# Late attention's transposed probabilities travel by way of a scratch in DRAM

## The chip, the cores and the metric

The kernel runs on one core of a Trainium2 chip. The metric is the device time of one execution in microseconds, the median of several runs. A core has a matmul engine (TensorE, PE in the profile; its weight loads are PEld), a vector engine (VectorE, DVE), a scalar engine (ScalarE, ACT), GpSimd (POOL) and SyncE (SP), which issues the transfers of this kernel. Each engine works through its own instructions in order; sixteen DMA engines move the data.

## What is computed

Attention over 4 batches, 8 heads, 576 positions and 64 dimensions a head. Half of the heads see the last 32 positions, the other half every 32nd position back. Two feed-forward layers follow; the second one sends each row to one of 8 experts.

```python
scores = scale * np.matmul(q, k.transpose(0, 1, 3, 2))
mask_local = (rel >= 0) & (rel < stride)                     # stride = 32
mask_strided = (rel >= 0) & (pos[None, :] % stride == pos[:, None] % stride)
scores = np.where(masks, scores, -1e9); attn = softmax(scores)
x = np.matmul(attn, v)                                       # to 2304 rows of 512
r = np.maximum(x @ w_in, 0.0)                                # 512 -> 2048
x = (s * (r * r) + b) @ w_out                                # 2048 -> 512
e_idx = np.argmax(x @ w_gate, axis=1)                        # one of 8 experts a row
out[row] = gate_w * eom * (np.maximum(x @ w1[e], 0.0) @ w2[e])
```

## The kernel before

The 2304 rows are worked in five units (256 and four times 512 rows). Attention is worked in 23 groups (GROUPS). The first nine are done by themselves; the other fourteen, "late attention", are woven into the first feed-forward layer of the first three units. These matmuls (L1095 into the hidden layer, L1129 out of it, with weights split into two parts and three passes) and those of late attention share TensorE.

The order of all instructions is written by a planner (class Order) when the program is built. Each piece of work is a generator that yields `op(engine and assumed time, what it waits for)`; the planner keeps a clock for each engine, picks the piece that can start first, with small penalties (P_ATT2 for attention, P_SPLIT2 for weights), and emits its instructions. All engines then run this order; only real waits move it in time. DMA counts as an engine with a clock of its own, and every DMA of these stages is issued by SP in the planned order. Tokens (Tok) stand for buffers, events (Ev) for data; an event that a transfer sets is assumed to come DMA_LAT (1.8 us) and a further constant after the transfer's assumed end.

A late group is one round. late_scores multiplies q and k, late_mask adds the mask into the tile pr, late_rest takes the maximum, the exponentials (L849, ScalarE) and the normalisation (L852 to L855, VectorE), and transposes 32x32 blocks from pr to prt (L859). The transposed blocks then have to go to other partitions: prt has 128 rows by (pair p of heads, half x of the queries, 32), phs needs 128 rows by (half x, block of keys y, 32). DMAs do that (L867): eight of 32 KB for a full round (nb = 2; groups L and T), four smaller ones for the two P groups (nb = 1). They wait for the token t_ph, that is for the former round's matmuls to have read phs, and the planner assumes 2.55 us times nb for them and DMA_LAT + PH_LAT = 2.6 us behind. Then one piece on TensorE holds the matmuls of phs with v (L884) and the scores of the group after next (L799). Two groups are under way at any time (NPR = 2 tiles pr), but prt, phs, and the tiles of the loaded q and k and of v exist once. So the loads of the next q and k and of the next v (load_qkv, L592) start as soon as a round's matmuls on TensorE have been done, at about the time of the next round's transfers. The weights' loads (L950) are on the same queue until 134 us; stores and loads of later stages (L934, L1227 and L1228, L1245, L1263, L1520) follow.

ev_x of a unit is set when all of its attention has been done; the unit's first feed-forward matmuls wait for it. Where the planner expects TensorE to stand still for longer, it puts in matmuls of no use (filler, L2393).

Of the kernel before, what the change touches and what calls it, by code (L numbers as in the profile page):

```python
# [6 lines left out]
F32 = mybir.dt.float32  # L7
# [31 lines left out]
QB = 64  # L39
# [13 lines left out]
NPR = 2  # L53
QG = 32
NQE = 6
P_CHAIN = -0.35
P_ATT = -0.3
P_QKL = 0.1
P_SPLIT = 0.0
# [61 lines left out]
def dims(g):  # L121

    if GROUPS[g][0] == "L":
        return (QB, LK) if g < NEARLY else (QG, 2 * QG)
    j0, j1, r = part_of(g)
    if g >= NEARLY:
        return r * (j1 - j0), r * j1
    return r * (j1 - j0), QB if GROUPS[g][0] == "P" else r * j1


def span(g):
    kind, b, i0, n = GROUPS[g]
    if kind == "L":
        return b * S + i0 * QB, b * S + (i0 + n) * QB
    j0, j1, _ = part_of(g)
    return b * S + j0 * STRIDE, b * S + j1 * STRIDE
# [62 lines left out]
DMA_LAT = 1.8  # L199
LATE_LAT = 0.8  # L200
PH_LAT = 0.8
# [115 lines left out]
def op(*engs, waits=(), dep=True, on=(), late=0.0):  # L317
    return engs, waits, dep, on, late
# [6 lines left out]
def body(ctx, tc, qkv, w12, moe_s, moe_b, wg, e12, out):  # L325
    nc = tc.nc
# [5 lines left out]
    dram = enter(tc.tile_pool(name="dram", bufs=1, space=DRAM))  # L332
# [23 lines left out]
    prs = [at.tile([P, 1024 // 2], F32, name=f"pr{k}", tag=f"pr{k}", bufs=1) for k in range(NPR)]  # L356
    prt = at.tile([P, 1024 // 2], F32, name="prt", tag="prt", bufs=1)
    phs = at.tile([P, 2, 2, 256], F32, name="phs", tag="phs", bufs=1)
    away = at.tile([P, 2, USZ[AWAY]], F32, name="away", tag="away", bufs=1)
    mh = wp.tile([P, sum(MB[0])], F32R, name="mh", tag="w")  # L360
    x0 = wp.tile([P, KD, USZ[0]], F32, name="x0", tag="w")
# [33 lines left out]
    o = Order()  # L395
# [68 lines left out]
    t_qe, t_qk, t_vv, t_pt, t_ph = Tok(NQE), Tok(1), Tok(1), Tok(1), Tok(1)  # L464
# [108 lines left out]
    for g, (kind, b, i0, n) in enumerate(GROUPS):  # L573
        t0, t1 = span(g)
# [26 lines left out]
    def attn(g):  # L601
# [41 lines left out]
        if g + 1 < len(GROUPS):  # L643
            o.spawn(attn(g + 1), prio=P_ATT if g + 1 < NFIRST else P_ATT1 if g + 1 < NEARLY else P_ATT2, pe=P_ATT)
        m = 2 * n
# [158 lines left out]
    def late_mask(g, sc, toks):  # L804
        kind, b, i0, n = GROUPS[g]
        local = kind == "L"
        nq, w = dims(g)
        m = 2 * n
        sm = at.tile([P, 24], F32, name="sm", tag="sm", bufs=NSM)
        ps4 = prs[g % NPR][:, 0:m * 2 * QG].rearrange("p (h i k) -> p h i k", h=2, k=2 * QG)[:, :, :, 0:w]  # L810
        edge = [i for i in range(n) if local and (i0 + i) % NLB == 0]
        some = [(i, i + 1, ml[:, 2 * QG:4 * QG]) for i in edge]
        for i, j in zip([0] + [i + 1 for i in edge], edge + [n]):
            if i < j:
                some.append((i, j, ml[:, 0:2 * QG] if local else late_m[kind, b]))
        yield op(("DVE", m * w / 960 + 0.15 * len(some)), on=toks)
        for i, j, mask in some:
            nc.vector.tensor_tensor(out=ps4[:, :, i:j], in0=sc[:, :, i:j], in1=mask.unsqueeze(1).unsqueeze(1).to_broadcast([P, 2, j - i, w]), op=ALU.add)
        o.spawn(late_rest(g, sm, ps4), prio=P_ATT2, pe=P_ATT)

    def attn_late(g):
# [4 lines left out]
        if g + 1 < NEARLY + NPR:  # L826
            o.spawn(attn(g + 1), prio=P_ATT2, pe=P_ATT)
        yield from late_mask(g, sc, toks)
# [3 lines left out]
    def late_rest(g, sm, ps4):  # L832
        kind, b, i0, n = GROUPS[g]
        local = kind == "L"
        nq, w = dims(g)
        m = 2 * n
# [8 lines left out]
        for h in range(2):  # L845
            for i in range(n):
# [10 lines left out]
        nb = 2 if w > QG else 1  # L857
        yield op(("DVE", nb * m * QG / 960 + 0.15), waits=[t_pt])
        nc.vector.transpose(out=prt[:, 0:nb * m * QG].rearrange("p (b c q) -> p b c q", b=nb, q=QG),  # L859
                            in_=pr[:, 0:m * 2 * QG].rearrange("p (c b q) -> p b c q", b=2, q=QG)[:, 0:nb])  # L860
        o.free(t_p)
        yield op(("DMA", 2.55 * nb), waits=[t_ph])
        for x in range(2):
            for y in range(nb):
                for p in range(2):
                    a, r = p * QB + x * QG, x * QB + y * QG
                    nc.sync.dma_start(out=phs[r:r + QG, p, x, 0:m * QG], in_=prt[a:a + QG, y * m * QG:(y + 1) * m * QG])  # L867
        t1 = o.fin + DMA_LAT + PH_LAT
        o.free(t_pt, t1)
        ev = Ev()  # L870
        o.set(ev, t1)
        tot = m * nq
# [7 lines left out]
        for i in range(n):  # L880
            for p in range(2):
                for h in range(2):
                    c = (h * n + i) * QG
                    nc.tensor.matmul(out=two[h * D:(h + 1) * D, p, 256 + 2 * i * nq:256 + 2 * (i + 1) * nq], lhsT=vv[:, i, p, h, :],  # L884
                                     rhs=phs[:, p, :, c:c + nq])
        o.free(t_vv)
        o.free(t_ph)
        if nx:
# [3 lines left out]
        for t0, c, z, _ in segs:  # L892
            if local:
                a = t0 - span(g)[0]
# [7 lines left out]
        for z, src, dst, u in runs:  # L902
            if u == AWAY:
# [9 lines left out]
                if local:  # L913
                    a = span(g)[0] - UOF[AWAY]
# [123 lines left out]
    def chain(k, u, h, ev, box):  # L1038
        U = USZ[u]
        held = k < CUT  # L1040
        yield op(("ACT", U / 1200 + 0.18), waits=[t_r] + ([t_w] if held and k % 3 == 0 else []))
        r = mx.tile([P, UMAX], F32, name="r", tag="r", bufs=NR)[:, 0:U]
        nc.scalar.activation(out=r, in_=h, func=AF.Relu)  # L1043
        to = r
        if held:
            if k % 3 == 0:
                plain[k // 3] = wp.tile([P, 3, U + 2], F32, name="gw", tag="w")
                nc.gpsimd.memset(plain[k // 3][:, :, U:U + 2], 1.0)
            gt = plain[k // 3][:, k % 3, :]
            to = gt[:, 0:U]  # L1050
        yield op(("DVE", U / 960 + 0.15), ("ACT", U / 1200 + 0.19, P_SQ))
        if o.eng == "DVE":
            nc.vector.tensor_tensor(out=to, in0=h, in1=r, op=ALU.mult)
        else:
            nc.scalar.activation(out=to, in_=r, func=AF.Square)  # L1055
        o.free(t_l1)
        if held:
            o.free(t_r)
            box.append(gt)
            o.set(ev)  # L1060
            return
        yield op(("ACT", U / 1200 + 0.19), waits=[t_g])
        gt = mx.tile([P, 2, UMAX], F32R, name="g", tag="g", bufs=NG)
        if u == CU:
            nc.gpsimd.memset(gt[:, 0, U:U + 2].bitcast(F32), 1.0)
            nc.gpsimd.memset(gt[:, 1, U:U + 2].bitcast(F32), 0.0)
        nc.scalar.activation(out=gt[:, 0, 0:U], in_=r, func=AF.Copy)  # L1067
        yield op(("DVE", U / 960 + 0.15))
        nc.vector.tensor_sub(out=gt[:, 1, 0:U], in0=r, in1=gt[:, 0, 0:U].bitcast(F32))  # L1069
        o.free(t_r)  # L1070
        box.append(gt)
        o.set(ev)
# [4 lines left out]
    def moe1():  # L1077
        def first_layer(k, u, fc):
# [22 lines left out]
            ev, box = Ev(), []  # L1101
            o.spawn(chain(k, u, h, ev, box), prio=P_CHAIN)
            return u, fc, ev, box
# [67 lines left out]
    def run(n):  # L1171
        while n and todo[1] is not None:
            yield todo[1]
            todo[1] = next(todo[0], None)
            n -= 1
# [184 lines left out]
    def combine1(u, q, hn, bank, box, m, r, ev0, ev1):  # L1360
# [8 lines left out]
        def c11():  # L1369
            yield op(("SP", 0.0), waits=[m["M2"]], dep=False)  # L1370
            yield op(("ACT", hn / 1200 + 0.2))
            nc.scalar.activation(out=rr[:, 0], in_=bank["a"], func=AF.Relu)
            o.free(t_l1)
            yield from square(rr[:, 0], rr[:, 0], hn)
            yield op(("SP", 0.0), waits=[t_g])
            g = mx.tile([P, 2, UMAX], F32R, name="g", tag="g", bufs=NG)
            box[0].append(g)
            yield from high_low(rr[:, 0], g[:, :, 0:hn], hn)

        def c12():  # L1380
            yield op(("DVE", w), waits=[m["M3"]], dep=False)
            nc.vector.tensor_tensor(out=rr[:, 1], in0=bank["c"], in1=su[:, 1], op=ALU.add)
            o.free(t_l1)
            o.free(t_su)
            yield from square(rr[:, 1], rr[:, 1], hn)
            yield from high_low(rr[:, 1], box[0][0][:, :, hn:2 * hn], hn)
            o.free(t_rr)
            o.set(ev0)
# [3 lines left out]
        o.set(r["u2"])  # L1392
        o.spawn(c11(), prio=P_CHAIN)
        yield op(("DVE", w), waits=[m["M7"]])
# [4 lines left out]
        o.set(r["c22"])  # L1399
        o.spawn(c12(), prio=P_CHAIN)  # L1400
        yield op(("DVE", w), waits=[m["M4"]])
# [10 lines left out]
    def both_rows(k, u, fc, prev):  # L1412
# [41 lines left out]
        yield from product("M6", "S2", "T2", "b", [t_l1], True)  # L1454
        o.spawn(combine1(u, q, hn, bank, box, m, r, ev0, ev1), prio=P_CHAIN)
        yield from run(1)
# [429 lines left out]
    def combine(hn, ps3, box, m, r, done):  # L1886
# [11 lines left out]
        def c11():  # L1898
            yield op(("SP", 0.0), waits=[m["M2"]], dep=False)
            yield from rise(a, h0, 0, hn, done["h0"])  # L1900
            o.free(t_l1)
# [16 lines left out]
        o.set(r["c22"])  # L1918
        o.spawn(c11(), prio=P_CHAIN)
        o.spawn(c12(), prio=P_CHAIN)  # L1920
        yield op(("DVE", w), waits=[m["M4"]])
# [474 lines left out]
    with tc.manual_schedule():  # L2396
# [4 lines left out]
        o.spawn(load_w64(0), after=False)  # L2401
        o.spawn(attn(0), prio=P_ATT, after=False)
        o.spawn(masks(1), after=False)
# [106 lines left out]
```

## Time and profile before

| | us |
|---|---|
| median of 3 runs | 662.09 (661.8 to 662.46) |
| the profiled execution | 662.37 |
| its span in the trace | 660.60 |
| TensorE busy in it | 651.9 |
| VectorE / ScalarE / GpSimd busy | 426.6 / 312.8 / 38.8 |
| late attention's transfers (L867), first and last issue | 72.5 and 245.8 |

The profile is one execution on the core. All times in it are microseconds from the start of the span; the profiled execution's own time has 1.77 us around the span. A row of the timeline has the start, the length and the engine, and merges like instructions that follow one another (x12). The length of a merged row runs to the end of its last instruction, so the pace is read from start to start.

### The profile page before, as it was taken

What the parts mean: (1) busy time and instruction counts of PE and PEld (TensorE: products, weight loads), DVE (VectorE), ACT (ScalarE), POOL (GpSimd) and SP (SyncE); (2) the same over time, 40 slices, a digit from 0 to 9 for tenths busy, and PEclk for the clock granted to TensorE, in tenths of its full rate; (3) what the DMA queues carried; (4) which work ended last, traced back from release to release, by engine and by line L of the source; (5) the groups of instructions that cost most, each with busy time, mean ns of one, the idle gap of its engine ahead of it and who ended that gap; (6) DMA issues with size and microseconds to landing.
All of it is one profiled execution on the core that took longest, in us unless ns stands there. A gap on an engine that the chain in (4) does not pass through costs nothing. (4 is left out here: it accounts for less than half of the span.)

```text
span 660.6 us, 14155 instructions
## 1 busy us (share of the span) xinstructions
PE 651.9 (99%) x5424; PEld 570.0 (86%) x5424; DVE 426.6 (65%) x1001; ACT 312.8 (47%) x848; POOL 38.8 (6%) x135
## 2 busy tenths in 40 slices
PE   7999999999999999999999999999999999999997
PEld 6888888899878888898899889988899999998996
DVE  5898868776545557566575767887687566535540
ACT  4876865677566444353243464543322423314311
POOL 7650000000000000000000000000000000000000
PEclk9999999999999999999999999999999999999999
DMA  8982356673544232112211242333220660910201
GB/s 312 405 334 96 112 209 208 207 245 103 177 152 169 81 106 65 49 48 97 87 50 42 64 152 68 116 97 96 96 65 2 177 237 14 327 44 16 81 1 66
DMA packets 40823, 83.81 MB, mean 127 GB/s; under 512 B 6701, under 2 KB 20142, under 8 KB 39986
## 3 DMA queue, kind: packets, MB, share of 16 engines
q1 hardware_dynamic: 40658, 82.87, 37.2%
q8 instruction: 43, 0.70, 0.5%
q14 instruction: 26, 0.21, 0.1%
q0 software_dynamic: 96, 0.02, 0.0%
HBM read 64.11 MB, written 15.63 MB: 121 GB/s over the span
## 5 line engine op out<-in xcount | busy, mean ns | idle before, releaser
L1095 PE MATMUL h<-xsl,w 128*128 128x512 f32 (+1 forms) x492 | 109.5, 369 | 0.0
L1129 PE MATMUL bk<-g,w 128*128 128x512 f32 (+1 forms) x480 | 105.5, 368 | 0.0
L1190 PE MATMUL bk<-g,w 128*128 128x512 f32 x396 | 102.2, 393 | 0.0
L1095 PEld LDWEIGHTS h<-xsl,w 128*128 128x128 f32 x492 | 84.8, 188 | 15.6 <-issue 0.4
L1968 PE MATMUL bk<-w,ht 128*128 128x512 f32 x384 | 96.0, 391 | 0.0
L1129 PEld LDWEIGHTS bk<-g,w 128*128 128x128 f32 x480 | 83.0, 188 | 14.7
L1190 PEld LDWEIGHTS bk<-g,w 128*128 128x128 f32 x396 | 69.9, 188 | 11.6
L1968 PEld LDWEIGHTS bk<-w,ht 128*128 128x128 f32 x384 | 68.6, 188 | 11.6
L1043 ACT ACTIVATE r<-h 128x512 f32<-128x512 f32 (+1 forms) x48 | 25.3, 528 | 62.5 <-PE h L1095 59.5
L1069 DVE TENSOR_TENSOR g<-r,g 128x512 fp32r<-128x512 f32 (+1 forms) x41 | 26.0, 633 | 42.6 <-ACT g L1067 42.2
L1442 PEld LDWEIGHTS h<-xsl,w 128*128 128x128 f32 x336 | 45.5, 190 | 3.8 <-issue 0.2
L1442 PE MATMUL h<-xsl,w 128*128 128x256 f32 x336 | 47.0, 283 | 0.0
L1873 ACT ACTIVATE ht<-h 128x256 fp32r<-128x256 f32 x24 | 9.2, 385 | 73.2 <-PE h L2010 47.0
L849 ACT ACTIVATE pr<-pr,sm 128x64 f32<-128x64 f32 (+2 forms) x102 | 32.8, 322 | 0.3
L1914 DVE TENSOR_TENSOR dd<-h,su 128x256 f32<-128x256 f32 x16 | 6.8, 424 | 29.5 <-PE h L2010 29.4
L1356 ACT ACTIVATE g<-dd 128x512 fp32r<-128x512 f32 x16 | 10.1, 631 | 31.5 <-DVE dd L1349 31.5
L1067 ACT ACTIVATE g<-r 128x512 fp32r<-128x512 f32 (+1 forms) x41 | 23.9, 583 | 1.7
L1055 ACT ACTIVATE r<-r 128x512 f32<-128x512 f32 (+1 forms) x41 | 23.9, 584 | 1.1
L2010 PE MATMUL bk<-x,wc 128*128 128x256 f32 x168 | 24.4, 281 | 0.0
L1442 PE MATMUL h<-xsl,s 128*128 128x256 f32 x168 | 24.3, 279 | 0.0
L1442 PEld LDWEIGHTS h<-xsl,s 128*128 128x128 f32 x168 | 22.6, 188 | 1.3
L1938 ACT ACTIVATE ob<-bk,scl 128x512 f32<-128x512 f32 x17 | 11.7, 689 | 23.5 <-PE bk L1968 22.8
(306 smaller groups left out, 1132.7 us busy)
## 6 DMA issues: line engine op xcount, KB each, us to landing
raw<-w SPq DMA_DIRECT2D x32, 512.0 KB, 6.9
qkv<-qkv SPq DMA_DIRECT2D x14, 512.0 KB, 4.7
xr<-xd SPq DMA_DIRECT2D x9, 512.0 KB, 4.7
qkv<-qkv SPq DMA_DIRECT2D x8, 544.0 KB, 6.3
out<-ob SPq DMA_DIRECT2D x17, 256.0 KB, 2.1
xd<-x SPq DMA_DIRECT2D x4, 1024.0 KB, 4.2
sraw<-sd SPq DMA_DIRECT2D x16, 256.0 KB, 2.7
wraw<-e SPq DMA_DIRECT2D x16, 256.0 KB, 3.0
```

The lines of the kernel that those rows point to most:

```text
L849: nc.scalar.activation(out=ps4[:, h, i, :], in_=ps4[:, h, i, :], func=AF.Exp, scale=0.125, bias=v[2][:, j:j + 1], accum_out=v[1][:, j:j + 1])
L1043: nc.scalar.activation(out=r, in_=h, func=AF.Relu)
L1055: nc.scalar.activation(out=to, in_=r, func=AF.Square)
L1067: nc.scalar.activation(out=gt[:, 0, 0:U], in_=r, func=AF.Copy)
L1069: nc.vector.tensor_sub(out=gt[:, 1, 0:U], in0=r, in1=gt[:, 0, 0:U].bitcast(F32))
L1095: nc.tensor.matmul(out=h, lhsT=w_t[2 * fc][:, a, c * P:(c + 1) * P], rhs=xt(u, c, x), start=(c == 0 and n == 0), stop=(c == KD - 1 and n = ...
L1129: nc.tensor.matmul(out=acc[pu][c], lhsT=w_t[2 * pf + 1][:, a, c * P:(c + 1) * P], rhs=gt[:, x, 0:cols(pu)], start=(first and n == 0), stop ...
L1190: nc.tensor.matmul(out=acc[pu][c], lhsT=w_t[2 * pf + 1][:, a, c * P:(c + 1) * P], rhs=pbox[0][:, x, 0:cols(pu)], start=(begin and i == 0), ...
L1442: nc.tensor.matmul(out=out_, lhsT=weights(x, a, c), rhs=o_place(u, b)[y][:, c], start=(first and c == 0 and n == 0), stop=(name in ("M2", ...
L1938: nc.scalar.activation(out=ob, in_=src, func=AF.Copy, scale=scl[:, i:i + 1])
L1968: nc.tensor.matmul(out=acc2[s, t][0], lhsT=box[k][:, x, t * P:(t + 1) * P], rhs=w_t["p", 2 * f + 1][:, a, :], start=(f == 0 and n == 0), s ...
L2010: nc.tensor.matmul(out=banks[to], lhsT=t[:, a, off + c * P:off + (c + 1) * P], rhs=x2[s, b][:, y, c, :], start=(first and c == 0 and n == ...
```

## The change

The blocks go from prt to a scratch tile in DRAM (one for each of the two tiles pr) by two writes, one for each pair of heads, and from there to phs by four reads (two for a P group). The two indices in phs change places, and the matmul reads it accordingly. The writes wait for nothing but the transposed tile; prt is given free when the writes have landed; the reads wait for them and for t_ph. The planner's assumed times are new: 0.75 us for the writes and RB = 1.5 us for the reads, each with DMA_LAT + 0.3 us behind.

```diff
+RB = 1.5
...
+    ptd = [dram.tile([2, QG, 2, 2, 256], F32, name=f"ptd{k}") for k in range(NPR)]
...
         o.free(t_p)
-        yield op(("DMA", 2.55 * nb), waits=[t_ph])
+        yield op(("DMA", 0.75))
+        pd_ = ptd[g % NPR]
+        c = m * QG
+        for p in range(2):
+            nc.sync.dma_start(out=pd_.rearrange("x k b p c -> (x k) b p c")[:, 0:nb, p, 0:c],
+                              in_=prt[p * QB:(p + 1) * QB, 0:nb * c].rearrange("q (b c) -> q b c", b=nb))
+        t1 = o.fin + DMA_LAT + 0.3
+        o.free(t_pt, t1)
+        ev = Ev()
+        o.set(ev, t1)
+        yield op(("DMA", RB), waits=[t_ph, ev])
         for x in range(2):
-            for y in range(nb):
-                for p in range(2):
-                    a, r = p * QB + x * QG, x * QB + y * QG
-                    nc.sync.dma_start(out=phs[r:r + QG, p, x, 0:m * QG], in_=prt[a:a + QG, y * m * QG:(y + 1) * m * QG])
-        t1 = o.fin + DMA_LAT + PH_LAT
-        o.free(t_pt, t1)
+            for b in range(nb):
+                nc.sync.dma_start(out=phs[x * QB + b * QG:x * QB + (b + 1) * QG, x, :, 0:c], in_=pd_[x, :, b, :, 0:c])
+        t1 = o.fin + DMA_LAT + 0.3
...
-                                     rhs=phs[:, p, :, c:c + nq])
+                                     rhs=phs[:, :, p, c:c + nq])
```

## Rows read from the trace of the kernel before

**Rows 1.** The page, part 1: busy time, share, instructions of TensorE.

```profile
PE   651.9 (99%) x5424; PEld 570.0 (86%) x5424; DVE 426.6 (65%) x1001; ACT 312.8 (47%) x848; POOL 38.8 (6%) x135
```

**Rows 2.** Windows: stretch, its length, busy time by engine, clock, DMA share, GB/s.

```profile
0.00:30.00 30.00, 26.09 (x356) 22.00 (x360) 21.08 (x46) 19.29 (x78) 21.33 (x73) 0.94 0.95 354
30.00:640.00 610.00, 610.00 (x4973) 533.78 (x4974) 402.09 (x949) 289.96 (x766) 16.65 (x62) 1.00 0.36 118
70.00:250.00 180.00, 180.00 (x1920) 151.18 (x1918) 115.41 (x241) 110.64 (x347) 1.17 (x18) 1.00 0.49 159
640.00:660.60 20.60, 15.84 (x101) 14.24 (x99) 3.39 (x8) 3.51 (x6) 0.86 (x1) 0.98 0.15 53
```

**Rows 3.** Timeline of TensorE: start, length, line, operation, tiles, count.

```profile
76.29 2.88 PE L1129 MATMUL bk<-g,w 128*128 128x512 f32 x12
79.01 2.88 PE L1095 MATMUL h<-xsl,w 128*128 128x512 f32 x12
81.82 1.15 PE L884 MATMUL bk<-phs,qkv 128*64 128x64 f32 x32
...
123.26 1.15 PE L884 MATMUL bk<-phs,qkv 128*64 128x64 f32 x32
...
136.68 1.15 PE L884 MATMUL bk<-phs,qkv 128*64 128x64 f32 x32
...
176.06 1.15 PE L884 MATMUL bk<-phs,qkv 128*64 128x64 f32 x32
...
201.86 1.15 PE L884 MATMUL bk<-phs,qkv 128*64 128x64 f32 x32
```

**Rows 4.** L867 in three rounds: SP ns min/median/max, first and last issue; landing.

```profile
L867 SPq DMA_DIRECT2D phs<-prt x8: 507/555/592, 127.4 to 133.0; - x8
DMA to landing us min/median/max: 1.8/3.9/5.7
...
L867 SPq DMA_DIRECT2D phs<-prt x8: 507/585/589, 166.9 to 172.0; - x8
DMA to landing us min/median/max: 1.8/4.0/5.3
...
L867 SPq DMA_DIRECT2D phs<-prt x8: 518/588/589, 192.4 to 196.8; - x8
DMA to landing us min/median/max: 1.8/1.9/1.9
```

**Rows 5.** Loads on SP ahead; landing of the second transfer at 127.41 and 166.94.

```profile
124.45 1.01 SPq L592 DMA_DIRECT2D qkv<-qkv  x2
166.03 0.81 SPq L592 DMA_DIRECT2D qkv<-qkv  x2
...
DMA to landing us min/median/max: 4.8/4.8/4.8
DMA to landing us min/median/max: 5.0/5.0/5.0
```

**Rows 6.** Other transfers between DRAM and SBUF by line, as in rows 4.

```profile
L1228 SPq DMA_DIRECT2D sd<-sr x8: 422/424/447, 202.8 to 290.6; - x8
DMA to landing us min/median/max: 2.0/2.2/5.9
L1263 SPq DMA_DIRECT2D sraw<-sd x16: 319/320/332, 255.0 to 438.7; - x16
DMA to landing us min/median/max: 2.0/2.0/2.9
```

**Rows 7.** Timeline of VectorE: the transpositions of two rounds.

```profile
126.18 0.71 DVE L859 STREAM_TRANSPOSE prt<-pr 128x512 f32<-128x512 f32 x1
143.15 0.71 DVE L859 STREAM_TRANSPOSE prt<-pr 128x512 f32<-128x512 f32 x1
```

**Rows 8.** Timeline of TensorE at the filler matmuls of L2393.

```profile
294.57 0.76 PE L2393 MATMUL bk<-xsl 128*128 128x256 f32 x5
295.17 1.57 PE L1190 MATMUL bk<-g,w 128*128 128x512 f32 x6
```

## The prediction

> **What bounds the kernel now.** I read the page first: TensorE is busy for 651.9 of 660.6 us [rows 1]. Then the windows, to see where the other 8.7 us lie: 3.9 us before 30 us and 4.8 us after 640 us; between them TensorE is never idle, and the granted clock is 1.00, which is the 2.4 GHz level [rows 2]. A busy TensorE may still hide waits, so the third view is its timeline, read from start to start. Twelve 128x512 matmuls take 2.72 us (76.29 to 79.01), and 2.81 us when a round of late attention follows (79.01 to 81.82) [rows 3]. So late attention (about 60 to 250 us) is woven into a dense stream of feed-forward matmuls. It is not the bound. Making its transfers quicker shortens nothing by itself; making them late stops TensorE, since a round's matmuls stand at a fixed place in its program.
>
> That place is set by the kernel's planner with assumed times. A round's eight transfers are assumed to take 2.55 x 2 + 1.8 + 0.8 = 7.7 us from the first issue. The trace gives the real time and so the room left before the matmuls of L884. In the round at 127.41 the last issue is at 133.0 and lands 1.8 us later, at 134.8; L884 starts at 136.68: room 1.9 us. At 166.94: 172.0 + 1.8 = 173.8 against 176.06, room 2.3. At 192.44: 196.8 + 1.8 = 198.6 against 201.86, room 3.3 [rows 3, 4]. The other nine of the twelve full rounds, read in the same way, have 1.5 to 6.3 us. So today the real transfers always beat their place.
>
> The same rows show a second thing. When nothing is ahead of them, all eight land within 1.8 to 1.9 us (192.44). Where two 512 KB loads of q, k and v stand just ahead on SP (124.45, 166.03), the slowest of the eight lands after 5.3 to 5.7 us, the second of them still after 4.8 to 5.0, the quickest, which is the last, after 1.8 [rows 4, 5]: the first ones wait behind the loads' bytes, and the long row of issues (4.4 to 5.6 us from first to last) hides that. In ten of the twelve full rounds the slowest takes 4.1 us or more.
>
> **The change part by part.** *Removed:* eight transfers of 32 KB in each of 12 full rounds and four smaller ones in two rounds, 104 in all; one costs SP 0.51 to 0.59 us and they stand about 0.67 us apart [rows 4]. *Added:* two writes to DRAM and, after a wait on them, four reads (two in the small rounds), 80 in all. SP gains 24 x 0.67 = 16 us of issue time over 190 us; SP bounds nothing, so that is worth 0.
>
> *The writes.* The trace has no such write; the nearest rows are sd (0.42 us of SP, landing 2.0 us where it is undisturbed) and today's transfers (0.51 to 0.59 us and 0.67 from start to start) [rows 4, 6]. I take 0.6 us from first to second, nearer to today's because these too cover a part of the partitions, and 0.2 us more to land than a transfer into SBUF (2.0 against 1.8).
>
> *The reads.* The nearest row is sraw<-sd, 0.32 us of SP and 2.0 us to land; the upper bound is today's 0.59 us and the 2.2 us of sd [rows 4, 6]. With 0.08 us between issues, three gaps and a landing give 3 x 0.40 + 2.0 = 3.2 to 3.0 x 0.67 + 2.2 = 4.2 us; I take 3.6, the middle, because a quarter of the partitions is what today's dear ones have and DRAM on one side is what the cheap ones have.
>
> *The wait between them* is the point. SP stands until both writes have landed; behind it are the loads of q, k, v for the next round, until 134 us those of the weights, and later those of sd. A hold of 2 us in front of them is hidden today, since TensorE waits for none of these loads in this stage [rows 2]; without that cover it would cost its own length in each round. But the writes now meet the loads ahead of them in full, and nothing hides it. Ready times of the three rounds with the change put in the same place:
> At 127.41: 127.4 + 0.6 + 4.8 (the second transfer's landing) + 0.2 + 3.6 = 136.6, 1.8 us later than now. At 166.94: 166.9 + 0.6 + 5.0 + 0.2 + 3.6 = 176.3, 2.5 later. At 192.44: 192.4 + 0.6 + 1.9 + 0.2 + 3.6 = 198.7, 0.1 later [rows 4, 5].
> Meanwhile the planner assumes 0.75 + 2.1 + 1.5 + 2.1 = 6.45 us instead of 7.7 and so puts the round's matmuls 1.25 us earlier. The room becomes 1.9 - 1.8 - 1.25 = -1.15, 2.3 - 2.5 - 1.25 = -1.45 and 3.3 - 0.1 - 1.25 = +1.95 us. A round whose writes stand behind loads stops TensorE for some 1.3 us, any other not at all.
>
> That a DRAM write lands only 0.2 us later than one into SBUF is this trace's [rows 4, 6]. The Trainium skill, "DMA: Bandwidth & Descriptors", section on the anatomy of one DMA, puts most of a fixed 2 us on the receipt of the write and says the delay can be long above all where the target is HBM; the rows agree on the 2 us and not on a surcharge. By that page of the Trainium skill two trips in series would have 4 us of fixed cost, an estimate; a receipt 1 us longer than the rows' would lengthen each stop by that.
>
> *What moves the other way.* The writes need only the transposed tile, no longer the free place in phs; only the reads wait for that. Where the transposition is done well before the former round's matmuls, the writes go ahead of the loads and are hidden, and the reads are issued like today's third and fourth transfer; room stays. Today the transposition ends up to 5 us behind the former round's matmuls (143.15 + 0.71 against 136.68 + 1.87), in five of eleven rounds by 0 to 2 us (126.18 + 0.71 against 123.26 + 1.78) [rows 3, 7], where loads are still under way. With the planner's rounds now bound by the softmax chain, the two chains drift against each other. A write meets fresh loads if it comes within some 4 us after them, of a round of about 12 us: a third of 12 rounds, so 3 or 4. Attention then ends earlier, which at best spares the five filler matmuls at 294.57, 0.60 us [rows 8].
> *Nothing:* the matmuls read phs in another order of the same 64 columns; VectorE, ScalarE and GpSimd have the same instructions. The extra 3.2 MB written go beside a DMA share of 0.49 in that stage [rows 2].
>
> **Sum.** 3.5 rounds x 1.3 us = 4.6, less 0.6 where the fillers go: about +4 us. The profiled execution is 662.37 us, its span of 660.60 and 1.77 around it, 0.28 above the median of 662.09. Span about 664.6, median 666.
>
> **Rivals.** *The decoupling keeps every write ahead of the loads* (not slower). Place: the SP queue in each round. For it: prt is freed as soon as the writes land instead of at the end of the round, so transpositions can run ahead; every round has 1.5 us or more of room today; a round that is not behind loads keeps 2 us. Against it: the softmax chain ends just behind the former round in those five of today's rounds. It decides where at most one write meets loads: 0 to 1.3 us, less 0.6. Time 662.1.
> *All loaded rounds stay loaded:* ten rounds x 1.2 us = 12 us, 674 us. For it: today's ten of twelve. Against it: that phase comes from the wait for phs, which the writes lose.
> *A gain:* the planner's order behind 250 us comes out shorter; the only idle time is 4.8 us at the end and the fillers' 0.6 us [rows 2, 8]. To show, it has to take 0.7 us from the end besides the fillers; nothing in late attention leads there. 660.7 us.
>
> **How the numbers follow.** I give the forecast (two to six rounds stop, 664 to 669 us) 0.50, the heavy case 0.10, no loss 0.35, a gain 0.05. About 0.2%, 1.3 us, is what a measurement of this kernel tells from no change. Faster 0.05, same 0.35, slower 0.60. The range takes in the case without loss down to 661.3, and 670 at the top, where reads at the upper bound (0.6 us more in each of four rounds) still lie; 0.05 is left out below and about 0.08 above. The forecast's own range is 664 to 669.
>
> **What would show it.** In the profile after: start-to-start gaps above 2.81 us ahead of L884, in rounds whose writes follow qkv loads by under 4 us, about 1.3 us each and none elsewhere; in those rounds writes that land after 4 us or more, SP standing for that time; rounds closer together, the last before 245 us. Wrong: TensorE as dense as before in every round (then the writes ran ahead), stops in rounds with quick writes (then the reads or the loads of v are the late ones), or a change in time that lies behind 250 us.

## The result and the profile after

The changed kernel takes 666.11 us (median, 665.1 to 667.91) against 662.28 us (661.8 to 662.53) for the kernel before: 1.0059 times as long, 95% interval 1.0044 to 1.0074, or 3.8 us more. The profiled execution of the changed kernel took 666.21 us, its span 664.4 us. The forecast of 666.0 us met the total. Its working did not: less than half of what it put on late attention is there, and another part of the 3.8 us lies at the last store, where the prediction expected nothing.

The part of the page that answers to [rows 1], and the windows of the kernel after that answer to [rows 2] (stretch, length, busy us and instructions of TensorE, its weight loads, VectorE, ScalarE and GpSimd, granted clock, DMA share, GB/s):

```profile
PE 651.7 (98%) x5424; PEld 569.2 (86%) x5424; DVE 426.5 (64%) x1003; ACT 312.1 (47%) x846; POOL 39.2 (6%) x135
...
0.00:30.00 30.00, 25.69 (x376) 21.39 (x376) 21.51 (x47) 19.66 (x81) 22.09 (x74) 1.00 0.95 353
30.00:640.00 610.00, 607.62 (x4940) 531.16 (x4932) 401.02 (x947) 288.92 (x760) 16.27 (x60) 1.00 0.38 124
70.00:250.00 180.00, 178.32 (x1911) 149.65 (x1910) 116.06 (x243) 110.55 (x345) 1.17 (x18) 1.00 0.56 179
640.00:664.40 24.40, 18.41 (x119) 16.64 (x117) 3.97 (x9) 3.51 (x6) 0.87 (x1) 0.93 0.13 45
```

TensorE has as much to do as before (651.7 against 651.9 us). It is no longer dense between 30 and 640 us: 607.62 of 610, so 2.4 us idle, of which 1.7 lie between 70 and 250 us. The list of TensorE's waits names them (us in total, times, longest):

```profile
PE bk L893 <- DMA phs<-ptd: 1.6, 2, 1.1
PE bk L2250 <- DMA we<-e: 0.7, 1, 0.7
```

L893 is L884 of before, the matmul of a late round. The timeline of TensorE after, to be held against [rows 3] (idle time before it and its releaser in brackets; L1104 and L1138 are L1095 and L1129 of before, and L2402 is the filler, L2393 of before):

```profile
114.54 1.52 PE L1138 MATMUL bk<-g,w 128*128 128x512 f32 x6
117.17 1.15 PE L893 MATMUL bk<-phs,qkv 128*64 128x64 f32 x32 [1.11 <-DMA phs<-ptd]
...
156.37 1.15 PE L893 MATMUL bk<-phs,qkv 128*64 128x64 f32 x32 [0.53 <-DMA phs<-ptd]
...
241.50 0.45 PE L893 MATMUL bk<-phs,qkv 128*64 128x64 f32 x8
...
296.06 0.76 PE L2402 MATMUL bk<-xsl 128*128 128x256 f32 x5
...
583.74 1.06 PE L2250 MATMUL bk<-we,xe 128*32 128x128 f32 x26 [0.71 <-DMA we<-e]
```

Two rounds of late attention stop TensorE, by 1.11 and 0.53 us. The last round starts at 241.50 us, against 249.53 before. The fillers that [rows 8] show are still there.

What SP does around the first stop, from its timeline, and its reads in that round and in one that nothing disturbs (SP ns min/median/max, first and last issue, then us to landing):

```profile
103.64 1.16 SPq L868 DMA_DIRECT2D ptd<-prt  x2
107.03 1.02 SPq L594 DMA_DIRECT2D qkv<-qkv  x2
108.10 0.42 SPq L959 DMA_DIRECT2D raw<-w  x1
108.83 2.48 SPq L877 DMA_DIRECT2D phs<-ptd  x4
...
L877 SPq DMA_DIRECT2D phs<-ptd x4: 324/566/878, 108.8 to 110.4; - x4
DMA to landing us min/median/max: 7.0/7.3/7.3
...
L877 SPq DMA_DIRECT2D phs<-ptd x4: 342/422/424, 190.2 to 191.5; - x4
DMA to landing us min/median/max: 1.8/1.9/1.9
```

The two writes (L868) went out at 103.64. Before the four reads (L877) the planner put two loads of q, k, v and one of weights. The reads were then issued at 108.8 to 110.4. Three of them have a landing on record, 7.0 to 7.3 us later, the last of these at 116.8; the fourth has none, and TensorE starts at 117.17. The second of the writes, issued at 104.20, took 4.6 us to land, until 108.8; SP had come to the reads by 108.52, so its delay cost 0.2 to 0.3 us and the delay of the reads some 5. A load of instructions runs there, too (queue q8, at 110.07), but for 0.88 us only. With nothing ahead of them, in the round at 190.2, they land in 1.9 us. All writes and all reads of the kernel:

```profile
L868 SPq DMA_DIRECT2D ptd<-prt x28: 473/578/650, 72.0 to 234.8; - x28
DMA to landing us min/median/max: 1.8/2.4/4.6
...
L877 SPq DMA_DIRECT2D phs<-ptd x52: 324/419/1755, 75.4 to 237.1; - x52
DMA to landing us min/median/max: 1.6/2.7/7.3
```

So the writes, which the prediction had behind the loads, mostly ran ahead of them: 2.4 us in the middle, and over 3.4 us in three rounds only (104.2, 122.4 and 129.4 us). The reads met the loads instead.

The second stop is of another kind. SP issued nothing between its writes (148.61 and 149.19 us, landed after 2.8 and 2.5 us) and its reads, whose row follows, with the load of instructions that the DMA queues show in the 2.5 us from 153 us:

```profile
L877 SPq DMA_DIRECT2D phs<-ptd x4: 331/414/1755, 151.7 to 153.0; - x4
DMA to landing us min/median/max: 1.8/3.2/3.4
...
q8 instruction: 1, 0.02, 3.5%
```

From the first write to the last landing (156.23 us) this round took 7.6 us, where the planner had assumed 6.45; the round at 190.2, which nothing disturbs, took about 6.2 (its fourth read has no landing on record and is taken at 1.9). One read held SP for 1.755 us, from 153.04, and the load of instructions runs from 153.04 for 1.39 us.

**Where the 3.8 us are.** I divide both profiled executions at the same four events: the first scores of late attention, the first matmul of the next stage (L1442, after the change L1451), the start of VectorE's last instruction, the end of the span.

| | before | after | difference |
|---|---|---|---|
| to the first scores of late attention | 60.8 | 60.3 | -0.5 |
| from there to the first L1442 / L1451 | 224.6 | 226.6 | +2.0 |
| from there to VectorE's last instruction | 370.56 | 371.62 | +1.1 |
| from there to the end | 4.68 | 5.86 | +1.2 |
| span | 660.6 | 664.4 | +3.8 |

The first and the third difference are of kinds that change from one execution to the next: the first stage waits for q, k, v by varying amounts, and the third holds the 0.7 us wait for the expert weights (583.74), which does not come back when the same kernel runs again (370.49 us in e1_again). The second and the fourth do come back, as 1.7 and 1.5 us in e1_again. The last one is a store. Its rows, before and after (L2077 and L2086, SP ns, first and last issue; landing):

```profile
L2077 SPq DMA_DIRECT2D out<-ob x2: 333/333/333, 653.5 to 656.5; - x2
DMA to landing us min/median/max: 1.7/1.7/1.7
...
L2086 SPq DMA_DIRECT2D out<-ob x2: 332/332/332, 656.1 to 659.0; - x2
DMA to landing us min/median/max: 2.9/2.9/2.9
```

The same 128 KB store takes 1.7 us before and 2.9 us after (after, only the second of the two stores has a landing on record), and no other transfer of data runs beside it. The DMA queues in the two microseconds from 659 us of the kernel after (packets, MB, share), and in the stretch of before that holds its last store:

```profile
q1 hardware_dynamic: 138, 0.13, 19.1%
q8 instruction: 1, 0.02, 3.6%
...
q1 hardware_dynamic: 144, 0.13, 9.6%
q14 instruction: 2, 0.02, 1.4%
```

After the change a load of instructions, one packet of 0.02 MB on queue q8 at 659.57 us, falls between the issue of the last store and its landing. Before, the nearest one on that queue is at 652.9 us, 3.0 us ahead of VectorE's last instruction and 3.5 us ahead of the store's issue. (The smaller packets of q14 come at the end of both.)

The packets also show where the 1.2 us go. The store has 144: 128 of 1 KB, and 16 of 4 bytes. The stretch of before from 657.2 to 657.9 us, then those of after from 659.8 to 660.4 and from 660.4 to 661.6:

```profile
q1 hardware_dynamic: 144, 0.13, 55.1%
...
q1 hardware_dynamic: 135, 0.12, 60.2%
...
q1 hardware_dynamic: 9, 0.01, 4.0%
```

Before, all 144 start within 0.5 us. After, 135 do, and the other nine, a sixteenth of the store (eight of 1 KB and one of 4 bytes), come one by one from 660.73 to 661.42; the load of instructions took 1.17 us from 659.57, so it ended at 660.73. That fits a load that keeps one of the sixteen DMA engines, and with it that engine's share of the store; the records do not name the engine.

### The profile page after: what moved, and what is told of

It is laid out like the page before. It is cut to its first block, busy times and chain, and to the rows that moved or that the text cites. A ratio compares the mean times of both kernels' runs of the same rounds, so it can differ in the third digit from the quotient of the medians.

```text
span 664.4 us, 14087 instructions
## 1 busy us (share of the span) xinstructions
PE 651.7 (98%) x5424; PEld 569.2 (86%) x5424; DVE 426.5 (64%) x1003; ACT 312.1 (47%) x846; POOL 39.2 (6%) x135
## 5 line engine op out<-in xcount | busy, mean ns | idle before, releaser
L1104 PE MATMUL h<-xsl,w 128*128 128x512 f32 (+1 forms) x492 | 108.7, 369 | 0.0
L1138 PE MATMUL bk<-g,w 128*128 128x512 f32 (+1 forms) x480 | 106.2, 368 | 0.0
L1104 PEld LDWEIGHTS h<-xsl,w 128*128 128x128 f32 x492 | 84.9, 188 | 15.5 <-issue 0.2
L1138 PEld LDWEIGHTS bk<-g,w 128*128 128x128 f32 x480 | 82.9, 188 | 14.9 <-issue 0.2
L1451 PEld LDWEIGHTS h<-xsl,w 128*128 128x128 f32 x336 | 45.5, 190 | 3.8 <-issue 0.2
L1451 PE MATMUL h<-xsl,w 128*128 128x256 f32 x336 | 47.0, 283 | 0.0
L1451 PE MATMUL h<-xsl,s 128*128 128x256 f32 x168 | 24.3, 279 | 0.0
L1451 PEld LDWEIGHTS h<-xsl,s 128*128 128x128 f32 x168 | 22.6, 188 | 1.3
```

The source lines that it names most:

```text
L1104: nc.tensor.matmul(out=h, lhsT=w_t[2 * fc][:, a, c * P:(c + 1) * P], rhs=xt(u, c, x), start=(c == 0 and n == 0), stop=(c == KD - 1 and n = ...
L1138: nc.tensor.matmul(out=acc[pu][c], lhsT=w_t[2 * pf + 1][:, a, c * P:(c + 1) * P], rhs=gt[:, x, 0:cols(pu)], start=(first and n == 0), stop ...
L1451: nc.tensor.matmul(out=out_, lhsT=weights(x, a, c), rhs=o_place(u, b)[y][:, c], start=(first and c == 0 and n == 0), stop=(name in ("M2", ...
```

## The experiments

Three questions. What stops TensorE in late attention: the new route (two trips in series), or the earlier place that the planner gives the round, since it assumes 6.45 us instead of 7.7? What slows the last store: where the scratch lies in DRAM, the length of SP's program, or the load of instructions? And is there a rest? All of them in one table; the ratio is against the kernel before on the same chip. "Stops" is TensorE's time waiting for phs in the profiled execution, "store" the landing of the last store there.

| kernel | median us | ratio, 95% interval | stops us | store us |
|---|---|---|---|---|
| after | 666.11 | 1.0059 [1.0044, 1.0074] | 1.6 | 2.9 |
| e1_again | 665.55 | 1.0049 [1.0032, 1.0067] | 1.4 | 3.2 |
| e4_place | 665.64 | 1.0050 [1.0032, 1.0069] | 1.6 | 2.7 |
| e3_early | 665.11 | 1.0035 [1.0015, 1.0054] | 0 | 1.7 |
| e3_look | 664.79 | 1.0029 [1.0015, 1.0043] | 1.2 | 1.7 |
| e2_late | 663.84 | 1.0021 [1.0007, 1.0035] | 0 | 3.1 |
| e5_scratch | 661.97 | 0.9987 [0.9974, 1.0000] | 0 | not recorded |
| e7_home | 666.11 | 1.0052 [1.0028, 1.0075] | 0.8 | 2.7 |
| e8_both | 664.32 | 1.0030 [1.0014, 1.0045] | 0 | 2.6 |
| e9_pad | 672.64 | 1.0151 [1.0122, 1.0180] | 0 | 2.9 |
| e11_after_pad | 674.49 | 1.0179 [1.0151, 1.0207] | 0.9 | 2.8 |
| e10_nofill | 662.02 | 0.9991 [0.9979, 1.0003] | 0 | 1.7 |
| e12_pecode | 663.15 | 1.0004 [0.9993, 1.0014] | 0 | 1.7 |

**The changed kernel again (e1_again).** No edit.

> The changed kernel once more. Theory A (TensorE stops ahead of the matmuls of phs): the same two rounds stop again, near 117 and 156 us, by 0.4 to 1.8 us each and 1.5 to 3 us together; median 665.5 to 666.5. Theory B (half of the loss lies behind 250 us, where the order is the same as before): the wait for the expert's weights (0.7 us near 583) and the slow landing of the last store (2.9 in place of 1.7 us) come again, 1.5 to 2.5 us together. If neither of the two later losses comes again, they are chance of one execution.

The same two rounds stop, by 0.91 us (at 117.97) and 0.48 us (at 156.98), and the last store takes 3.2 us; the wait for the expert weights is gone. The stops and the store belong to the program, the wait for the weights does not.

**The new route in the old place (e4_place).** The planner's plan is that of before; only the transfers, the scratch and the order of columns in phs are exchanged.

```diff
-        for x in range(2):
-            for y in range(nb):
-                for p in range(2):
-                    a, r = p * QB + x * QG, x * QB + y * QG
-                    nc.sync.dma_start(out=phs[r:r + QG, p, x, 0:m * QG], in_=prt[a:a + QG, y * m * QG:(y + 1) * m * QG])
+        for p in range(2):
+            nc.sync.dma_start(out=pd_.rearrange("x k b p c -> (x k) b p c")[:, 0:nb, p, 0:c],
+                              in_=prt[p * QB:(p + 1) * QB, 0:nb * c].rearrange("q (b c) -> q b c", b=nb))
+        for x in range(2):
+            for y in range(nb):
+                nc.sync.dma_start(out=phs[x * QB + y * QG:x * QB + (y + 1) * QG, x, :, 0:c], in_=pd_[x, :, y, :, 0:c])
```

> The new route in the very place of the eight transfers and planned with their old times, so that TensorE, ScalarE, VectorE and GpSimd keep the order of before. The prediction's sums: the round at 127.4 is ready 1.8 us later, that at 166.9 2.5 later, that at 192.4 0.1 later, against rooms of 1.9, 2.3 and 3.3: stops of at most 0.5 us in two or three rounds, 662.3 to 663.3. Theory B: no stops, but the wait for the expert's weights and the slow last store show up, 663.8 to 664.8. Theory C: stops of over 1 us in several rounds, 665 or more.

This is the kernel for which the prediction worked out its ready times, before it moved the matmuls. SP's timeline around one of its rounds, the landing of that round's writes and reads (L867, L871), and TensorE's timeline at that round and the other one that stops:

```profile
167.02 1.54 SPq L593 DMA_DIRECT2D qkv<-qkv  x2
168.61 1.17 SPq L867 DMA_DIRECT2D ptd<-prt  x2
174.51 1.72 SPq L871 DMA_DIRECT2D phs<-ptd  x4
...
DMA to landing us min/median/max: 5.3/5.4/5.5
DMA to landing us min/median/max: 1.9/1.9/1.9
...
153.06 1.15 PE L888 MATMUL bk<-phs,qkv 128*64 128x64 f32 x32 [0.84 <-DMA phs<-ptd]
...
177.92 1.15 PE L888 MATMUL bk<-phs,qkv 128*64 128x64 f32 x32 [0.80 <-DMA phs<-ptd]
```

Here the writes do stand behind two loads, land after 5.3 to 5.5 us, and SP issues nothing from 169.8 to 174.5 us. The reads then land at 175.8 + 1.9 = 177.7 us. In the other two rounds of the prediction they are there at 134.2 + 1.9 = 136.1 and 198.6 + 2.1 = 200.7 us. Forecast were 176.3 for this round, 136.6 and 198.7. The route alone costs 1.6 us of stops without any earlier place, and 3.1 us in all, 1.0 of it at the store (2.7 us against 1.7). That is more than the prediction's sums left for it (stops of at most 0.5 us, 662.3 to 663.3).

**The old route in the early place (e3_early, e3_look).** The kernel before with the planner told that its eight transfers take 1.25 us less. e3_look is the same kernel once more, for a second profile.

```diff
-        yield op(("DMA", 2.55 * nb), waits=[t_ph])
+        yield op(("DMA", 2.55 * nb - 1.25 * (nb - 1)), waits=[t_ph])
```

> The kernel before with its eight transfers, but planned 1.25 us shorter in full rounds (6.45 us). Theory A says that a round stops where the room is used up: the least room is 1.5 us, so the shift alone leaves 0.25 us or more in every round: no stop, 662.0 to 662.9. If the earlier place alone does it: stops in two or more rounds, 664 to 666. Theory B (scratch in DRAM and its traffic): no change here, 662.3.

> The kernel before with its eight transfers planned 1.25 us shorter, once more, since its times fell into two groups (662.2 to 662.5 and 663.8 to 667.7) and the profile shown was of the first group, without a stop but with rooms down to 0.2 us (round at 167.24), 0.6 and 0.7. If small rooms and the scatter of landings make the second group: a profile of 664 or more shows stops at those rounds, 2 to 4 us together. If it is something else: no stop there, the time is lost before 60 or behind 285 us.

The first profile is of an execution of 662.49 us, 2.6 us under its kernel's median of 665.11: no stop, and as little as 0.2 us of room in the tightest round. The second profile is of one of 665.92 us. TensorE's waits there, and its timeline in the round that stops:

```profile
PE bk L799 <- DMA qkv<-qkv: 1.3, 1, 1.3
PE bk L884 <- DMA phs<-prt: 1.2, 2, 1.0
...
159.50 0.34 PE L884 MATMUL bk<-phs,qkv 128*64 128x64 f32 x4 [0.95 <-DMA phs<-prt]
160.07 1.03 PE L884 MATMUL bk<-phs,qkv 128*64 128x64 f32 x28 [0.23 <-DMA phs<-prt]
```

So the earlier place alone costs 2.1 to 2.6 us with the old transfers, where the room of 1.5 us in the rows of before had led to expect no stop. Not only the transposed probabilities are then late (1.2 us) but the load of q and k for the scores as well (L799, 1.3 us). With rooms of 0.2, 0.6 and 0.7 us in three rounds of the first profile (0.6 in the round that stops in the second) the same program stops in one execution and not in the other.

**The new route in a later place (e2_late).** The changed kernel with 1.25 us added to the time that the planner assumes behind the reads, so that the round's total is 7.7 us again.

```diff
-        t1 = o.fin + DMA_LAT + 0.3
+        t1 = o.fin + DMA_LAT + 1.55
```

> The changed kernel with the planner told that the reads land 1.25 us later, so that the whole route is planned at 7.7 us as the eight transfers were. Theory A: the matmuls stand later, no round stops, median 662.0 to 662.9. Theory B: the stops go, the losses behind 250 us stay, 663.8 to 664.8. Theory C (the route itself is too slow however it is planned): stops remain in two or more rounds, 665 or more.

TensorE's waits in this kernel, the whole list:

```profile
PE warm L2389 <- DVE xsl L475: 1.4, 1, 1.4
PE bk L636 <- ACT x L758: 0.6, 1, 0.6
PE bk L641 <- DMA qkv<-qkv: 0.4, 1, 0.4
```

None of them is of late attention: the stops have gone, and from the first scores to the first L1451 it takes 224.5 us, as before the change. The median is 1.7 us under that of e1_again, which ran on the same chip, and 1.3 us over the kernel before (1.0021). These 1.3 us lie at the last store, which takes 3.1 us.

**Where the scratch lies (e5_scratch, e7_home, e8_both).** e5_scratch is the kernel before with the scratch tiles laid out in DRAM and written once each, by 16 KB that nothing reads, behind 500 us. e7_home is the changed kernel, and e8_both is e2_late, with the scratch in a tensor that the kernel before already has.

```diff
# e5_scratch
+    ptd = [dram.tile([2, QG, 2, 2, 256], F32, name=f"ptd{k}") for k in range(NPR)]
...
+        for t in ptd:
+            nc.sync.dma_start(out=t[0, :, 0, 0, 0:P], in_=ones[0:QG, :])
# e7_home, e8_both
-    ptd = [dram.tile([2, QG, 2, 2, 256], F32, name=f"ptd{k}") for k in range(NPR)]
+    ptd = [xd[AWAY].rearrange("a b c -> (a b c)")[k * 65536:(k + 1) * 65536].rearrange("(x k b p c) -> x k b p c", x=2, k=QG, b=2, p=2) for k in range(NPR)]
```

> The kernel before, with the two scratch tiles laid out in DRAM beside the others but used only once, by two transfers of 16 KB behind 500 us; nothing else differs in any engine's order. Theory B (what is laid out in DRAM makes the last store land 1.2 to 1.5 us later): last store 2.4 to 3.2 us in place of 1.7, median 663.5 to 664.2. If the layout does nothing: 1.7 us and 662.2 to 662.9, and the slow store belongs to the traffic of the route.

> The changed kernel with its scratch inside a DRAM tile that the kernel before has already (the last unit's rows, written only later), so that no new tile is laid out; same orders of TensorE, ScalarE, VectorE and GpSimd. Theory B: the last store lands after 1.7 us again, the stops ahead of the matmuls of phs stay: 664.0 to 664.8. If the slow store comes from the route's traffic: 665.5 as the changed kernel.

> Both remedies: the scratch inside the old DRAM tile and the reads planned 1.25 us later. Theories A and B together leave nothing of the loss: no stop, last store 1.7 us, 662.1 to 662.8. If either loss has another cause: 663.5 or more.

The scratch laid out but hardly used costs nothing (0.9987), with 4.6 us from VectorE's last instruction to the end (4.7 before). The scratch moved into a tensor that was there already gains nothing (666.11 and 664.32 us; stores of 2.7 and 2.6 us). The place of the scratch in DRAM is not the cause.

**The length of SP's program (e9_pad, e11_after_pad).** The change takes 24 transfers out of SP's program. These kernels put 24 back, of 16 KB each, which nothing reads, behind 500 us: e9_pad into e2_late, e11_after_pad into the changed kernel.

```diff
+        for n in range(24):
+            nc.sync.dma_start(out=ptd[n % 2][n // 2 % 2, :, n // 4 % 2, n // 8 % 2, n // 16 * P:n // 16 * P + P], in_=ones[0:QG, :])
```

> The kernel of e2 (reads planned 1.25 us later, no stops) with 24 further transfers of 16 KB on SP behind 500 us, which only bring SP's stream back to about the number of transfers that the kernel before has. Theory D (the last store waits for a load of SP's code that now falls on it, since SP's stream has another length): the code load moves off the store, which lands after 1.7 us again, 662.2 to 662.9. If the slow store comes from the route's traffic itself: 2.4 to 3.2 us as in e2, 663.6 to 664.3.

> The changed kernel with the same 24 transfers behind 500 us. Theories A and D: the stops of about 1.8 us near 117 and 156 us stay, the last store is quick: 664.0 to 665.0. If the slow store stays: 665.5 to 666.2.

The last store still takes 2.9 and 2.8 us. The length of SP's program is not the cause. The 24 transfers themselves cost 8 to 9 us, since they hold SP for 15.9 us, from 506.94, and what SP issues behind them is on the path, as TensorE's longest wait in e9_pad shows:

```profile
PE h L2019 <- DVE dd L1931: 7.1, 1, 7.1
```

TensorE stands from 520.8 us on, and the granted clock falls to 0.50, the 1.2 GHz level, at 524.9 us for 6.8 us: the first six 128x256 matmuls behind the wait take 1.45 us from start to start, where six take 0.71 at 1.00.

**The length of TensorE's program (e12_pecode).** A weight load or matmul that waits for several transfers has an instruction for each further semaphore ahead of it. A round used to wait for eight transfers and now waits for four. The instructions of this kind at L884 and L893 (engine, count, ns):

```profile
L884 PEldq EVENT_SEMAPHORE  x54: 51/51/1076, 78.5 to 247.1; - x54
...
L893 PEldq EVENT_SEMAPHORE  x31: 51/51/4991, 78.7 to 238.8; - x31
```

Matmuls, weight loads and these together, TensorE's program has 5424 + 5424 + 134 = 10982 instructions in the trace of before and 5424 + 5424 + 113 = 10961 in that of after, 21 fewer. Its instructions seem to be loaded a fixed number at a time: the 43 packets of q8 are of equal size, one for each 255 of the 10982. With fewer instructions each load then comes later against TensorE's work. e12_pecode is e2_late with one 64-column matmul, whose result is overwritten at once, in each of eleven rounds: with its weight load 22 instructions (five waits fewer leave 17 more in the trace, 10978).

```diff
+        if g < 20:
+            nc.tensor.matmul(out=two[:, 0, 256:320], lhsT=ident_r, rhs=mk[:, MW:MW + 64])
```

> The kernel of e2 (reads planned 1.25 us later, no stops) with one further matmul of 64 columns in each of eleven rounds of late attention, whose result is overwritten at once: 22 more instructions in TensorE's stream, which lost 21 with the four transfers a round less to wait for. Theory E (a load of TensorE's code of 16 KB falls on the last store since its stream has become shorter): the load comes back to about 3 us ahead of the last VectorE instruction, the last store lands after 1.7 us, the end of the span comes 4.6 to 4.8 us after that instruction's start in place of 5.6 to 6.3; median 663.84 - 1.3 + 11 x 0.1 = 663.2 to 664.0 with the matmuls' own cost. If another engine's stream is the one, VectorE's for instance: the store stays at 2.4 us or more and the median is 664.6 to 665.2.

The last store of e12_pecode (L2088), and the DMA queues between 653 and 654 us:

```profile
L2088 SPq DMA_DIRECT2D out<-ob x2: 332/332/332, 654.4 to 657.4; - x2
DMA to landing us min/median/max: 1.7/1.7/1.7
...
q8 instruction: 1, 0.02, 6.0%
```

The load of instructions is back at 653.6 us, 3.3 us ahead of VectorE's last instruction (656.87), and the store takes 1.7 us, with eleven matmuls more to do. The median is 663.15 us, 1.0004 [0.9993, 1.0014]. The other profiles agree: in the eight with the shorter program of TensorE (after, e1, e2, e4, e7, e8, e9, e11: 10960 or 10961 instructions) the load comes 1.0 to 1.7 us after the start of VectorE's last instruction, nine packets of the store come only when it has ended, and the store lands in 2.6 to 3.2 us; in before, e3_early, e3_look, e10 and e12 (10972 to 10984) the load comes 2.9 to 3.5 us ahead of it, all packets of the store start within 0.5 us, and it lands in 1.7 us (e5 has the load 3.4 us ahead and the packets within 0.5 us, and no landing). e10_nofill, below, has ten instructions fewer than before and is still quick, so it is not any change of length that does it.

**Without the fillers (e10_nofill).** The kernel before, with no filler matmuls in that stage.

```diff
-        if idle < (0.5 if ev_k[8].t is None else 1.2):
+        if idle < 0.5 or ev_k[8].t is not None:
```

> The kernel before without the five filler matmuls near 294.6 us. The prediction's term for them is 0.60 us: 661.6 to 662.1 where before has 662.5, if nothing else moves; if TensorE waits there anyway, no change.

0.9991 [0.9979, 1.0003]: a gain of 0.6 us (-0.2 to 1.4), the size of [rows 8], but not told apart from none.

## Why the total was right and its working was not

**What bounds the kernel** held. TensorE's work is unchanged, the 16 us that SP saves are worth nothing, and the extra bytes (DMA share 0.56 against 0.49 in that stage) cost nothing by themselves: e2_late moves them too, and late attention takes 224.5 us there against 224.6.

**The ready times** held roughly. Counted from the first write, the route takes 9.2, 9.1 and 6.4 us in those three rounds, against the 9.2, 9.4 and 6.3 us of the sums. In the place for which they were worked out (e4_place) the last reads are there 0.5 us earlier, 1.4 us later and 2.0 us later than forecast. The later two are those behind TensorE's stops, which push everything back: the writes went out 1.7 us (168.61 against 166.9) and 1.9 us later (194.31 against 192.4) than today's first transfers, with 0.84 and 1.64 us of stops ahead of them, and in the first of the two SP was held by the loads for 1.54 us instead of 0.81. The price of the writes on SP was right (0.58 us for 0.6), and the four reads take 1.3 + 1.9 = 3.2 us undisturbed, the lower bound of what the prediction gave (3.2 to 4.2, taken 3.6). The writes behind loads cost more than the sums had: 5.3 to 5.5 us where 5.0 to 5.2 was taken. One of the readings behind that is wrong [rows 5]: the 4.8 us at 127.41 is the landing of the third transfer (128.63); the second (127.99) has none on record. A write to DRAM lands in 2.4 us against 1.8 to 1.9 for the reads into SBUF: 0.5 to 0.6 us more, where the prediction took 0.2. The Trainium skill, "DMA: Bandwidth & Descriptors", section on the anatomy of one DMA, has the receipt of a write heaviest where it goes to HBM; that section is written for transfers issued by GpSimd, and these are SP's. The rows here agree with it on a surcharge, which the rows of before did not show.

**The step that failed** is "the writes go ahead of the loads and are hidden, and the reads are issued like today's third and fourth transfer; room stays", with the count behind it, "a third of 12 rounds, so 3 or 4". The first half came true more often than I put it. The second half did not: once the writes and the reads are two pieces of work, the planner puts the next loads between them, and the reads then wait behind the loads' bytes as the first transfers of [rows 4] did, up to 7.3 us, with no long row of issues to hide it. Two rounds stop, by 1.11 and 0.53 us, in place of 3.5 by 1.3: 1.6 us instead of 4.6. Of the two, the first is behind loads by its rows. The second has quick writes, which the prediction named as a sign against it, and no load between writes and reads. There two trips in series with one issue of 1.755 us took longer than the place allowed. A load of instructions begins with that issue, and in the same round of e1_again, e7_home and e11_after_pad, too, an issue of 1.36 to 1.45 us overlaps such a load and TensorE stops, by 0.27 to 0.48 us. No run takes the load away from this round and leaves the rest, so it is not shown to be the cause.

**What sets these stops** was named rightly: the place is planned 1.25 us earlier than the data allow. Give the round its 7.7 us back and they go (e2_late). Neither half is harmless by itself, though: the route alone stops TensorE for 1.6 us (e4_place), the place alone costs 2.1 to 2.6 us (e3), and both together give stops of 1.4 to 1.6 us (after, e1_again), not the sum. The planner lays the rounds out anew each time, so the parts need not add.

**What was not in the sum** is 1.2 us at the last store. The prediction named "a change in time that lies behind 250 us" as a sign against it; it is there. The rows behind it: the store and the load of instructions overlap in each profile where the store is slow; a longer program of TensorE, and nothing else changed, moves the load away and makes the store quick again (e12_pecode). The 16 KB on another queue slow the 128 KB by way of nine packets, which start only when the load has ended. The Trainium skill, "Runtime: NRT & Kernel Launch", section on instruction fetch mechanics, says that each engine's instructions come in blocks of 16 KiB by a DMA queue of its own and that crossing a block is mostly hidden. The trace agrees on the block (43 packets, 0.70 MB in the page's part 3) and, at the end of this kernel, not on the hiding: what pays is a store of another queue, by 1.2 us.

**The fillers** did not go, since the order behind 250 us is the same in both kernels; the -0.6 us is a second wrong term. By the parts of this profile that come back, the sum is 2.0 for late attention and 1.2 for the store, 3.2 us; the two measurements of the kernel gave 3.8 and 3.0 us. That the forecast met 666 is a chance of two errors: stops sized 3 us too large, less 0.6 for fillers that stayed, and a store that was not seen.

**The rivals.** "Every write keeps ahead of the loads" is nearest to what the writes do, and with the later place late attention costs nothing any more (e2_late); with the store quick as well the whole kernel is as fast as the one before (e12_pecode, 663.15 against 662.62 us). "All loaded rounds stay loaded" (674) fell, and so did the gain: no kernel here is shown to be quicker than the one before.

## What to carry to other kernels

When one step of transfers becomes two with a wait between them, look at what the scheduler may put between the two: the second trip pays for every load that slips in ahead of it. Fewer transfers and less issue time are worth nothing where the issuing queue is not the bound; the time assumed for the new route, and so the place of its consumer, decides. And after any edit that changes the number of instructions, look at the last microseconds for a load of instructions beside the last store before explaining a difference of a microsecond by the edit itself.

## What the runs showed of the hardware

A load of instructions (one packet of 0.02 MB, queue q8) between the issue and the landing of a 128 KB store goes with a landing of 2.6 to 3.2 us instead of 1.7, in eight profiles of eight; nine of the store's 144 packets then start only when the load has ended. Adding 22 instructions to TensorE's program was enough to move the load off the store (e12_pecode). Between 70 and 250 us, each of the nine transfers of the kernel before that took SP over 0.95 us to issue overlaps a load of instructions, and so do five of six in the kernel after. Reads of 1.9 us land in 7.0 to 7.3 us when two loads of q, k, v and one of weights were issued up to 1.8 us ahead of them. A write of this shape to DRAM lands 0.5 to 0.6 us later than the reads back from it.
